# Softmax sums' small constant added on GpSimd one step sooner, high parts of six weight pieces rounded on GpSimd

## The chip, the core and the metric

The kernel runs on one core of a Trainium2 chip. TensorE (PE in the rows) multiplies (PEld are its weight loads); VectorE (DVE), ScalarE (ACT) and GpSimd (POOL) work element by element, SyncE (SP) issues most loads. Each engine runs its own instructions strictly in the order of the program; between engines, semaphores hold an instruction until what it needs is there. The metric is the device time of one execution in microseconds, as a median of several runs. Before the change it is 601.28 us (601.18 to 601.39).

## The reference

Banded attention with a few global keys is followed by two gated products, all in float32:

```python
scores = scale * np.matmul(q, k.transpose(0, 1, 3, 2)) + bias     # 2 batches, 8 heads, 768 rows, 64 wide
scores = np.where(keep, scores, -1e9)
a = np.exp(scores - np.max(scores, axis=-1, keepdims=True))
a = a / (np.sum(a, axis=-1, keepdims=True) + 1e-09)
x = np.matmul(a, v)                                               # 1536 rows x 512
x = ((x @ w1) * (x @ w2)) @ w3 @ w_out                            # d_ff 1024
out = ((x @ w_a) * (x @ w_b)) @ w_out2                            # d_ff 1536
```

The line that matters here is the fifth: the small constant 1e-09 is added to the row sums before they divide.

## The kernel before

The 1536 rows are 12 tiles of 128. A *unit* is one tile and two heads, so attention has 48 units of 128 rows x 2 heads x 256 keys (128 keys in the first tile of a batch). `band_attention` runs a loop of *steps* `u`; in step `u` it emits, in this order, for different units (the lag behind `u` in brackets): the scores on TensorE (`band_scores`, every second step, two units), the exponentials on ScalarE with their row sums `z` (`band_exp`, unit `u-2`), transposes on TensorE with a copy on ScalarE (`band_turn`, five or six units behind), the products with v (`band_values`), and then, dealt out in turns by `feed`, the row maxima on VectorE (`band_max`, unit `u-1`, two instructions at line 444) and the normalisation (`band_norm`, unit `u-3`). Before the change `band_norm` has three parts: VectorE adds EPS to `z` (line 465, 128x2 numbers), VectorE takes the reciprocal (line 467), and GpSimd multiplies the exponentials by it (line 469, two instructions of 128x256). As a generator that stops after the addition, it comes in two turns: the addition follows the first maximum, the reciprocal the second.

The same loop feeds weights. They come as 64-bit floats in *pieces* of 128x512; a piece that is begun in step `s` gets two ScalarE instructions then (lines 89 and 90), three on VectorE in step `s+1` (lines 94, 98 and 102), its *high part* rounded on ScalarE in step `s+2` (`upper`, line 115), and its low part subtracted on VectorE in step `s+3` (line 119). Pieces are begun in steps 3, 6, 9, 12, 14, 16, 20 and 24, and every fourth step from 36 on. Every fourth step from 20 on prepares a tile of keys and queries: ScalarE rounds the keys (line 368), GpSimd the queries (line 369, 128x1024, tile `qa`), and one step later VectorE subtracts both (lines 380 and 383). Steps 2 to 5 also have GpSimd make two of the eight heads' bias tables each (line 321). From step 15 on, matrix products of the first expert (`ab_band`, lines 669 to 671) are put between the steps on TensorE; each ends with a copy on ScalarE (line 677) and a product on VectorE (line 678). No scheduler moves anything: the order in which the Python code emits the instructions is each engine's order.

A step in which VectorE has only its two maxima, the addition and the reciprocal is called *light* below: steps 16, 18, 20, 22, 24, 34, 36, 38, 40 and some more.

Of the kernel before, what the change touches and what calls it, by code (L numbers as in the profile page):

```python
# [14 lines left out]
ALU = mybir.AluOpType  # L15
# [6 lines left out]
EPS = 1.0e-9  # L22
# [5 lines left out]
def f32(ap):  # L28
    return ap.bitcast(F32)


class Emitter:
# [74 lines left out]
    def convert(self, hi, lo, raw, g=None):  # L107


        nc = self.nc  # L110
        g = self.half("g", list(hi.shape)) if g is None else g
        words, join = self.doubles(g, raw)

        def upper():
            nc.scalar.copy(out=hi, in_=g)
            yield

        def rest():
            nc.vector.tensor_tensor(out=lo, in0=g, in1=f32(hi), op=ALU.subtract)
            yield  # L120

        return [words, join, upper, rest]
# [328 lines left out]
    def band_exp(self, u):  # L451
# [7 lines left out]
            )  # L459
        self.sm[u] = (s, z, lo)  # L460

    def band_norm(self, u):
        nc = self.nc
        s, z, lo = self.sm[u]
        nc.vector.tensor_scalar_add(z, z, EPS)
        yield
        nc.vector.reciprocal(z, z)  # L467
        for j in range(2):
            nc.gpsimd.tensor_scalar(  # L469
                out=s[:, j, lo:], in0=s[:, j, lo:], scalar1=z[:, j : j + 1], scalar2=1.0, op0=ALU.mult, op1=ALU.mult  # L470
            )
# [51 lines left out]
    def band_attention(self, filler):  # L523

        self.v, self.qs, self.sp, self.sm, self.pt, self.pv = ({} for _ in range(6))
        self.kq = dict(enumerate(self.kq01))
        self.ks = self.const.tile([P, 3, self.H, P], F32R, name=self.name("ks"))
        self.globs = self.const.tile([P, self.H, MAX_GLOBAL], F32, name=self.name("globs"))
        C = self.C
        nt = self.B * self.NB  # L530
        nu = nt * C
        self.patient = True
        masks = self.band_masks()
        self.feed_load(1, self.nc.scalar)
        next(masks)

        self.nc.vector.tensor_copy(out=self.nf, in_=self.ni.bitcast(U32))
        next(masks)
        block_stages = (
            (0, self.band_load_v), (C - 1, self.band_global), (-3, self.band_low), (-4, self.band_high), (-6, self.band_load),  # L540
        )
        early = sorted((C * t + lag, t, n) for t in range(nt) for n, (lag, _) in enumerate(block_stages) if C * t + lag < 0)
        for _, t, n in early:
            if t and n != len(block_stages) - 1:
                for _ in block_stages[n][1](t) or ():
                    pass
        spent = 0.0
        turned = valued = 0
        stores = {}
        u = -1  # L550
        while self.stored < nt:
            u += 1
            self.step = u
            at = lambda lag, stage: stage(u - lag) if 0 <= u - lag < nu else None
            at(0, self.band_scores)
            at(2, self.band_exp)
            while turned < min(nu, u - 4 if u < 16 else u - 5):
                self.band_turn(turned)
                turned += 1


            while valued < min(nu, u - 5 if u < 16 else u - 6) and (u < self.pairs_from or u % 4 == 2):
                self.band_values(valued)
                valued += 1
                if valued % C == 0:
                    for n, stage in enumerate((self.store_x, self.store_x_low, self.set_stored)):
                        stores.setdefault(u + n, []).append((stage, valued // C - 1))
            turns = [at(1, self.band_max), at(3, self.band_norm)]
            turns += [stage(t) for stage, t in stores.pop(u, ())]
            for lag, stage in block_stages:  # L570
                t, c = divmod(u - lag, C)
                if c == 0 and 0 <= t < nt:
                    turns.append(stage(t))
            self.feed([x for x in turns if x])
            if u:
                next(masks, None)
            for _ in range(2):
                if spent < 0.85 * (u - 14) - 0.15 * max(u - 38, 0):
                    spent += next(filler)
        self.patient = False  # L580
# [918 lines left out]
```

## Time and profile before

| | us |
|---|---|
| median of three runs | 601.28 |
| the profiled execution | 600.37 |
| its span, first to last instruction | 598.5 |
| TensorE busy in the span | 581.9 |
| VectorE busy | 446.2 |
| ScalarE busy | 366.3 |
| GpSimd busy | 171.3 |

The profile is of one execution. Its time is 1.87 us longer than its span, and 0.91 us shorter than the median. Attention takes the first 120 us; in the rest of the span TensorE's products follow each other. A row of a timeline gives the start, the duration, the engine, the line, and in brackets the idle time of the engine before it with what ended it. Back to back, an instruction starts before the one in front of it has ended, so the distance of two starts, not the duration, is what an instruction takes of its engine.

### The profile page before, as it was taken

What the parts mean: (1) busy time and instruction counts of PE and PEld (TensorE: products, weight loads), DVE (VectorE), ACT (ScalarE), POOL (GpSimd) and SP (SyncE); (2) the same over time, 40 slices, a digit from 0 to 9 for tenths busy, and PEclk for the clock granted to TensorE, in tenths of its full rate; (3) what the DMA queues carried; (4) which work ended last, traced back from release to release, by engine and by line L of the source; (5) the groups of instructions that cost most, each with busy time, mean ns of one, the idle gap of its engine ahead of it and who ended that gap; (6) DMA issues with size and microseconds to landing.
All of it is one profiled execution on the core that took longest, in us unless ns stands there. A gap on an engine that the chain in (4) does not pass through costs nothing.

```text
span 598.5 us, 10290 instructions
## 1 busy us (share of the span) xinstructions
PE 581.9 (97%) x3632; PEld 507.8 (85%) x3632; DVE 446.2 (75%) x974; ACT 366.3 (61%) x802; POOL 171.3 (29%) x226
## 2 busy tenths in 40 slices
PE   6989999999999999999999999999999999999996
PEld 4678997888888888888899888888888888889996
DVE  6897989539967483739999777777777789984781
ACT  5998889747745473648664444444444465895830
POOL 5655767500000000422612022222222221555500
PEclk9999999999999999999999999999999999999999
DMA  8999683326424322796714012122220248999941
GB/s 231 283 250 239 161 214 104 113 72 208 140 71 142 124 88 70 141 231 126 109 28 141 34 54 79 47 70 71 72 71 2 71 136 220 235 143 191 195 99 57
DMA packets 31821, 76.78 MB, mean 128 GB/s; under 512 B 3601, under 2 KB 11281, under 8 KB 31761
## 3 DMA queue, kind: packets, MB, share of 16 engines
q1 hardware_dynamic: 20560, 57.42, 32.2%
q0 software_dynamic: 10624, 17.83, 18.0%
q10 hardware_dynamic: 576, 0.79, 0.5%
q8 instruction: 30, 0.49, 0.4%
q14 instruction: 31, 0.25, 0.1%
HBM read 55.05 MB, written 3.15 MB: 97 GB/s over the span
## 4 chain that ended last, share of the span: by engine, by line
PE 87%; DVE 6%; ACT 3%; issue 2%; POOL 1%; POOLq 0%; DVEq 0%; ACTq 0%
PE ab_band L931 29%; PE o_band L931 16%; PE y_band L931 10%; PE ab_band L669 7%; PE ab_band L670 6%; PE ab_band L671 6%; PE wfp_band L244 2%; PE wfp_band L243 2%; PE wfp_band L245 2%; PE pv_band L516 2%; DVE s_band L444 2%; PE pt_band L480 2%; ACT s_band L456 1%; DVE qb_band L383 1%; PE sp_band L410 1%
## 5 line engine op out<-in xcount | busy, mean ns | idle before, releaser
L931 PE MATMUL ab_band<-y_band,ws_band 128*128 128x512 f32 (+1 forms) x576 | 110.2, 337 | 0.0
L931 PEld LDWEIGHTS ab_band<-y_band,ws_band 128*128 128x128 f32 x576 | 91.1, 190 | 12.0
L669 PE MATMUL ab_band<-xh_band,w_band 128*128 128x512 f32 (+1 forms) x216 | 81.8, 379 | 0.0
L671 PE MATMUL ab_band<-xh_band,w_band 128*128 128x512 f32 (+1 forms) x216 | 79.1, 366 | 0.0
L670 PE MATMUL ab_band<-xl_band,w_band 128*128 128x512 f32 (+1 forms) x216 | 79.0, 366 | 0.0
L469 POOL TENSOR_SCALAR s_band<-s_band,z_band 128x256 f32<-128x256 f32 (+1 forms) x96 | 61.0, 648 | 35.9 <-DVE z_band L467 15.4
L931 PE MATMUL o_band<-wo_band,gs_band 128*128 128x256 f32 (+1 forms) x360 | 59.1, 326 | 0.0
L931 PE MATMUL y_band<-gs_band,wf_band 128*128 128x512 f32 (+1 forms) x336 | 58.4, 336 | 0.0
L931 PEld LDWEIGHTS o_band<-wo_band,gs_band 128*128 128x128 f32 x360 | 53.1, 190 | 5.9
L931 PEld LDWEIGHTS y_band<-gs_band,wf_band 128*128 128x128 f32 x336 | 51.8, 190 | 6.6
L931 PE MATMUL ab_band<-y_band,wa_band 128*128 128x512 f32 (+1 forms) x288 | 56.4, 338 | 0.0
L90 ACT ACTIVATE raw_band<-raw_band 128x512 int32<-128x512 uint32 x76 | 51.2, 674 | 0.0
L931 PEld LDWEIGHTS ab_band<-y_band,wa_band 128*128 128x128 f32 x288 | 46.0, 190 | 6.1
L678 DVE TENSOR_TENSOR g_band<-ab_band,b_band 128x512 f32<-128x512 f32 (+1 forms) x27 | 16.9, 629 | 45.2 <-ACT b_band L677 45.2
L456 ACT ACTIVATE s_band<-s_band,m_band 128x256 f32<-128x256 f32 (+1 forms) x96 | 46.8, 495 | 3.6 <-DVE m_band L444 3.4
L669 PEld LDWEIGHTS ab_band<-xh_band,w_band 128*128 128x128 f32 x216 | 40.7, 188 | 7.6 <-issue 1.0
L671 PEld LDWEIGHTS ab_band<-xh_band,w_band 128*128 128x128 f32 x216 | 40.6, 188 | 6.6
L670 PEld LDWEIGHTS ab_band<-xl_band,w_band 128*128 128x128 f32 x216 | 40.8, 189 | 6.1
L1133 ACT COPY p_band<-ab_band 128x512 f32<-128x512 f32 (+1 forms) x48 | 22.1, 484 | 33.2 <-PE ab_band L931 33.0
L799 POOL DMA_DIRECT2D wq_band<-wq_band x4 | 4.6, 1156 | 125.5 <-DVE wf_band L812 124.4
L1134 DVE TENSOR_TENSOR u_band<-ab_band,u_band 128x512 f32<-128x512 f32 (+1 forms) x24 | 13.3, 555 | 33.1 <-PE ab_band L931 32.6
L444 DVE CUSTOM_DVE_ANT_0 s_band<-sp_band,bias_band 128x256 f32<-128x256 f32 (+1 forms) x96 | 37.3, 391 | 0.6 <-ACT bias_band L309 0.4
(160 smaller groups left out, 1262.5 us busy)
## 6 DMA issues: line engine op xcount, KB each, us to landing
raw_band<-in_moe_w_dram SPq DMA_DIRECT2D x31, 512.0 KB, 4.8
raw_band<-in_moe_w_out_dram SPq DMA_DIRECT2D x20, 512.0 KB, 4.4
raw_band<-in_moe_w_b_dram SPq DMA_DIRECT2D x12, 512.0 KB, 3.5
raw_band<-in_moe_w_a_dram SPq DMA_DIRECT2D x12, 512.0 KB, 4.5
ga_band<-ga_band POOLq DMA_DIRECT2D x24, 256.0 KB, 6.8
v_band<-in_v_dram SPq DMA_DIRECT2D x12, 256.0 KB, 7.7
kd_band<-in_kq_dram SPq DMA_DIRECT2D x12, 256.0 KB, 6.6
qd_band<-in_kq_dram SPq DMA_DIRECT2D x12, 256.0 KB, 7.0
```

The lines of the kernel that those rows point to most:

```text
L90: nc.scalar.activation(out=low, in_=low.bitcast(U32), func=AF.Copy, scale=2.0**-29)
L243: nc.tensor.matmul(acc, w[:, 1, k % 4, :], o[:, 0, 0, :], start=(k == 0), stop=False)
L444: nc.vector.tensor_tensor_reduce(out=s[:, j, lo:], in0=sp[:, j, lo:], in1=bias[:, 2 * c + j, :], scale=-self.scale, scalar=FLT_MAX, op0=AL ...
L456: nc.scalar.activation(out=s[:, j, lo:], in_=s[:, j, lo:], func=AF.Exp, bias=m[:, j : j + 1], scale=-1.0, accum_out=z[:, j : j + 1],)
L469: nc.gpsimd.tensor_scalar(out=s[:, j, lo:], in0=s[:, j, lo:], scalar1=z[:, j : j + 1], scalar2=1.0, op0=ALU.mult, op1=ALU.mult)
L669: nc.tensor.matmul(p, wl, xh, start=(c == 0), stop=False)
L670: nc.tensor.matmul(p, wh, xl, start=False, stop=False)
L671: nc.tensor.matmul(p, wh, xh, start=False, stop=(c == self.C - 1))
L678: nc.vector.tensor_tensor(out=out[:, at], in0=ps[0], in1=b, op=ALU.mult)
L931: self.nc.tensor.matmul(bank, wt, xt, start=start and i == n == 0, stop=stop and n == 2 and i == len(terms) - 1, skip_group_check=more,)
L1133: copy = lambda out: nc.scalar.copy(out=out, in_=bank)
L1134: plus = lambda t: nc.vector.tensor_tensor(out=t, in0=bank, in1=t, op=ALU.add)
```

## The change

The addition of EPS becomes a method of its own, `band_sum`, on GpSimd, for unit `u-2` in step `u`: the step in which ScalarE makes that unit's sums, one step before the addition stood. `band_norm` is no longer a generator and is called before the turns are dealt out, so reciprocal and multiplications of unit `u-3` come first in step `u`, the addition for unit `u-2` behind them. In steps before 22 of the attention loop, `upper` rounds on GpSimd and not on ScalarE; by the steps in which pieces are begun these are the roundings of steps 5, 8, 11, 14, 16 and 18.

```diff
--- before.py
+++ after.py
@@ -112,7 +112,10 @@
         words, join = self.doubles(g, raw)
 
         def upper():
-            nc.scalar.copy(out=hi, in_=g)
+            if self.patient and self.step < 22:
+                nc.gpsimd.tensor_scalar(out=hi, in0=g, scalar1=1.0, scalar2=1.0, op0=ALU.mult, op1=ALU.mult)
+            else:
+                nc.scalar.copy(out=hi, in_=g)
             yield
 
         def rest():
@@ -459,11 +462,14 @@
             )
         self.sm[u] = (s, z, lo)
 
+    def band_sum(self, u):
+
+        _, z, _ = self.sm[u]
+        self.nc.gpsimd.tensor_scalar(out=z, in0=z, scalar1=EPS, scalar2=1.0, op0=ALU.add, op1=ALU.mult)
+
     def band_norm(self, u):
         nc = self.nc
         s, z, lo = self.sm[u]
-        nc.vector.tensor_scalar_add(z, z, EPS)
-        yield
         nc.vector.reciprocal(z, z)
         for j in range(2):
             nc.gpsimd.tensor_scalar(
@@ -565,7 +571,9 @@
                 if valued % C == 0:
                     for n, stage in enumerate((self.store_x, self.store_x_low, self.set_stored)):
                         stores.setdefault(u + n, []).append((stage, valued // C - 1))
-            turns = [at(1, self.band_max), at(3, self.band_norm)]
+            at(3, self.band_norm)
+            at(2, self.band_sum)
+            turns = [at(1, self.band_max)]
             turns += [stage(t) for stage, t in stores.pop(u, ())]
             for lag, stage in block_stages:
                 t, c = divmod(u - lag, C)
```

GpSimd's queue in steps 2 to 6, where `z` are row sums, `s` a unit's exponentials, `bias` the tables of the heads, and `w` a weight piece. Before:

```order
L321 TENSOR_SCALAR bias_band_230<-dist_band_227 128x256 x2
L469 TENSOR_SCALAR s_band_258<-s_band_258,z_band_271 128x128 x2
L321 TENSOR_SCALAR bias_band_230<-dist_band_227 128x256 x2
L469 TENSOR_SCALAR s_band_277<-s_band_277,z_band_283 128x128 x2
L321 TENSOR_SCALAR bias_band_230<-dist_band_227 128x256 x2
L469 TENSOR_SCALAR s_band_287<-s_band_287,z_band_315 128x128 x2
L321 TENSOR_SCALAR bias_band_230<-dist_band_227 128x256 x2
L469 TENSOR_SCALAR s_band_322<-s_band_322,z_band_335 128x128 x2
```

And now:

```order
L468 TENSOR_SCALAR z_band_271<-z_band_271 128x2
L324 TENSOR_SCALAR bias_band_230<-dist_band_227 128x256 x2
L475 TENSOR_SCALAR s_band_258<-s_band_258,z_band_271 128x128 x2
L468 TENSOR_SCALAR z_band_284<-z_band_284 128x2
L324 TENSOR_SCALAR bias_band_230<-dist_band_227 128x256 x2
L475 TENSOR_SCALAR s_band_278<-s_band_278,z_band_284 128x128 x2
L468 TENSOR_SCALAR z_band_316<-z_band_316 128x2
L324 TENSOR_SCALAR bias_band_230<-dist_band_227 128x256 x2
L475 TENSOR_SCALAR s_band_292<-s_band_292,z_band_316 128x128 x2
L468 TENSOR_SCALAR z_band_336<-z_band_336 128x2
L116 TENSOR_SCALAR w_band_296<-g_band_297 128x512
L324 TENSOR_SCALAR bias_band_230<-dist_band_227 128x256 x2
```

Each unit's addition stands behind the multiplications of the unit in front of it, and the next pair of tables, and once a rounding, behind the addition.

VectorE's queue from the end of step 37 to the start of step 40, where `m` are row maxima, `ks` keys, `xl` low parts of the attention's output. Before:

```order
L678 TENSOR_TENSOR g_band_933<-ab_band_1446,b_band_1603 128x512
L444 ISA s_band_1651,m_band_1652<-sp_band_1526,bias_band_230 128x256
L444 ISA m_band_1652 128x1
L465 TENSOR_SCALAR z_band_1574<-z_band_1574 128x2
L444 ISA s_band_1651,m_band_1652<-sp_band_1526,bias_band_230 128x256
L444 ISA m_band_1652 128x1
L467 RECIPROCAL z_band_1574<-z_band_1574 128x2
L394 CAST ks_band_221<-globs_band_222 128x8x32
L444 ISA s_band_1671,m_band_1672<-sp_band_1606,bias_band_230 128x256
L444 ISA m_band_1672 128x1
L465 TENSOR_SCALAR z_band_1616<-z_band_1616 128x2
L498 TENSOR_TENSOR xl_band_1159<-pv_band_1626,xh_band_1158 128x2x128
```

And now:

```order
L686 TENSOR_TENSOR g_band_934<-ab_band_1447,b_band_1604 128x512
L473 RECIPROCAL z_band_1575<-z_band_1575 128x2
L447 ISA s_band_1656,m_band_1657<-sp_band_1527,bias_band_230 128x256
L447 ISA m_band_1657 128x1
L447 ISA s_band_1656,m_band_1657<-sp_band_1527,bias_band_230 128x256
L447 ISA m_band_1657 128x1
L473 RECIPROCAL z_band_1617<-z_band_1617 128x2
L397 CAST ks_band_221<-globs_band_222 128x8x32
L447 ISA s_band_1676,m_band_1677<-sp_band_1607,bias_band_230 128x256
L447 ISA m_band_1677 128x1
L504 TENSOR_TENSOR xl_band_1164<-pv_band_1627,xh_band_1163 128x2x128
L122 TENSOR_TENSOR w_band_1558<-g_band_1559,w_band_1558 128x512
```

The reciprocal is now the first instruction of its step; the maxima of the step stand behind it.

ScalarE's queue in steps 5 and 6, where `pt` are transposed exponentials. Before:

```order
L456 ACTIVATE s_band_322,z_band_335<-s_band_322,m_band_323 128x128 x2
L482 COPY pt_band_341<-pt_band_338 128x2x128
L115 CAST w_band_295<-g_band_296 128x512
L456 ACTIVATE s_band_343,z_band_364<-s_band_343,m_band_344 128x256 x2
L482 COPY pt_band_370<-pt_band_367 128x2x128
```

Line 115's row is gone from there and from five more places; the rest of ScalarE's order, and all of TensorE's, is as it was.

## Rows read from the trace of the kernel before

**Rows 1.** Busy time in stretches: stretch, sum, then engines, PE clock, DMA share, GB/s.

```profile
30.00:45.00 15.00, 13.46 (x138) 11.48 (x136) 14.37 (x57) 14.85 (x46) 8.83 (x13) 1.00 1.06 252
...
75.00:90.00 15.00, 15.00 (x113) 13.47 (x111) 12.64 (x50) 13.24 (x41) 9.63 (x15) 1.00 0.86 213
...
120.00:150.00 30.00, 30.00 (x161) 24.98 (x160) 19.59 (x35) 18.63 (x34) 0.00 (x0) 1.00 0.41 136
```

**Rows 2.** The chain that ended last, in order of time: start us, us, what.

```profile
49.98 0.33 DVE s_band L444
...
79.52 0.33 DVE s_band L444
...
105.68 0.33 DVE s_band L444
...
106.17 0.63 PE pt_band L480 x4
```

**Rows 3.** Groups of instructions, line 465: count, busy us, mean ns, idle before.

```profile
L465 DVE TENSOR_SCALAR z_band<-z_band 128x2 f32<-128x2 f32 x48 | 11.3, 234 | 1.5 <-ACT s_band L456 1.5
```

**Rows 4.** Lines 465 and 467: count, duration ns min/median/max, first and last start.

```profile
L465 DVE TENSOR_SCALAR z_band<-z_band x48: 156/166/822, 9.6 to 116.1; 128x2 f32<-128x2 f32 x48
...
L467 DVE RECIPROCAL z_band<-z_band x48: 153/156/167, 10.0 to 116.3; 128x2 f32<-128x2 f32 x48
```

**Rows 5.** Timeline of POOL at the start: start us, us, engine, line, operation, shapes, count, idle.

```profile
8.98 0.89 POOL L321 TENSOR_SCALAR bias_band<-dist_band 128x256 bf16<-128x256 f32 x2 [0.57 <-DVE dist_band L317]
...
11.30 1.66 POOL L321 TENSOR_SCALAR bias_band<-dist_band 128x256 bf16<-128x256 f32 x2
...
12.95 0.72 POOL L469 TENSOR_SCALAR s_band<-s_band,z_band 128x128 f32<-128x128 f32 x2
```

**Rows 6.** Timeline of DVE, steps 7 and 8.

```profile
14.99 0.35 DVE L394 COPY kq<-globs_band 128x128 f32<-128x128 f32 x1
...
18.60 0.16 DVE L467 RECIPROCAL z_band<-z_band 128x2 f32<-128x2 f32 x1
```

**Rows 7.** Timeline of ACT, steps 2 to 12.

```profile
8.59 0.19 ACT L456 ACTIVATION_READ_ACCUMULATOR s_band<-s_band,m_band 128x1 f32 x1
...
20.22 0.51 ACT L456 ACTIVATE s_band<-s_band,m_band 128x256 f32<-128x256 f32 x1
...
26.27 0.64 ACT L115 CAST w_band<-g_band 128x512 fp32r<-128x512 f32 x1
...
26.79 0.52 ACT L456 ACTIVATE s_band<-s_band,m_band 128x256 f32<-128x256 f32 x1
```

**Rows 8.** Timeline of DVE, step 21.

```profile
49.55 0.42 DVE L678 TENSOR_TENSOR g_band<-ab_band,b_band 128x256 f32<-128x256 f32 x1 [4.02 <-ACT b_band L677]
```

**Rows 9.** Timeline of DVE, steps 38 to 41.

```profile
92.92 0.41 DVE L444 CUSTOM_DVE_ANT_0 s_band<-sp_band,bias_band 128x256 f32<-128x256 f32 x1
...
93.26 0.17 DVE L465 TENSOR_SCALAR z_band<-z_band 128x2 f32<-128x2 f32 x1
...
93.67 0.16 DVE L467 RECIPROCAL z_band<-z_band 128x2 f32<-128x2 f32 x1
...
93.75 0.28 DVE L394 CAST ks_band<-globs_band 128x256 fp32r<-128x256 f32 x1
...
95.42 0.41 DVE L444 CUSTOM_DVE_ANT_0 s_band<-sp_band,bias_band 128x256 f32<-128x256 f32 x1
...
98.12 1.47 DVE L380 TENSOR_TENSOR ks_band<-kd_band,ks_band 64x1024 fp32r<-64x1024 f32 x1
```

**Rows 10.** Timeline of POOL, steps 38 to 40.

```profile
94.03 0.93 POOL L469 TENSOR_SCALAR s_band<-s_band,z_band 128x256 f32<-128x256 f32 x2 [1.28 <-ACT s_band L456]
...
97.01 1.05 POOL L369 TENSOR_SCALAR qa_band<-qd_band 128x1024 fp32r<-128x1024 f32 x1
```

**Rows 11.** Timeline of ACT, steps 39 and 40.

```profile
95.88 0.51 ACT L456 ACTIVATE s_band<-s_band,m_band 128x256 f32<-128x256 f32 x1 [0.37 <-DVE m_band L444]
...
96.85 1.05 ACT L368 CAST ks_band<-kd_band 128x1024 fp32r<-128x1024 f32 x1
```

## Prediction

> **What bounds the kernel now.** I read the busy time by stretches first. From 120 to 150 us TensorE is busy for all of 30.00 us [rows 1], and so it goes on: what attention delays by then, the rest of the kernel does not give back. The change touches attention alone, the first 120 us. There no single engine is the bound: from 30 to 45 us ScalarE is busy for 14.85 us of 15 and VectorE for 14.37, from 75 to 90 us TensorE for 15.00 [rows 1]. GpSimd, at 8.83 and 9.63 us, has room on average. Second, the chain of waits. It runs through VectorE's maxima around 50 us and from 79.52 to 105.68 us for most of the time, and reaches TensorE for good at 106.17 us [rows 2]. So a microsecond of VectorE or ScalarE is worth something here, and the question is not how busy GpSimd is but when it hands the sums back. Third, therefore, the timelines of the places where the new order binds.
>
> **The addition leaves VectorE.** Its 48 instructions are busy 11.3 us, 156 ns at least and 822 ns at most [rows 3, 4]. Back to back one takes less of the queue: in step 38 addition and second maximum lie between 93.26 and 93.67 us, 0.41 us, of which a maximum takes 0.34 (92.92 to 93.26) [rows 9]; the addition's share is 0.07 us.
>
> **The addition on GpSimd.** The trace has no 128x2 operation of GpSimd. Its multiplications take 0.72 us for two of 128x128 [rows 5] and 0.93 us for two of 128x256 [rows 10], so 0.36 and 0.465 each; 128 columns more cost 0.105 us, and with no columns 0.255 us are left. I take 0.26 us; the ends are nothing and the 0.36 us of the nearest row. The moved rounding has 512 columns: between 0.465 us for 256 and 1.05 us for the 1024 of line 369 [rows 10], which gives 0.66 us.
>
> **The new circle.** In the new order the reciprocal of unit n waits for GpSimd's addition for n, which stands in GpSimd's queue behind the multiplications of unit n-1, which wait for the reciprocal of n-1. Nothing of this went round before: VectorE added by itself, and GpSimd could fall behind without VectorE noticing. One turn of the circle costs 0.36 us from a reciprocal's start to the multiplications' (93.67 to 94.03), 0.93 us for the multiplications [rows 9, 10] and 0.26 us for the addition: 1.55 us. A light step keeps VectorE for 0.83 us (92.92 to 93.75) [rows 9], and now for 0.07 less. Wherever VectorE sets the pace, the reciprocal behind a light step makes it wait, with all its queue: the next maxima, low parts and joins. In steps with two or more microseconds of other VectorE work the circle is covered.
>
> **Term 1, the start.** Here GpSimd is behind already, with the tables. From the end of unit 0's sums (8.59 + 0.19 = 8.78 us) [rows 7] until the addition for unit 4 it must do five additions (1.30 us), four pairs of tables at 0.89 us (3.56), the multiplications of units 0 to 3 at 0.72 us (2.88) [rows 5] and one rounding (0.66): 8.40 us, until 17.2 us. One pair of tables took 1.66 us instead of 0.89 while VectorE worked on a weight piece [rows 5]; with one such delay it is 18.0 us. VectorE's step 7, which began at 14.99 us [rows 6], now begins with the reciprocal of unit 4, so it is 3.0 us late. It reached the end of step 8 at 18.60 + 0.08 us [rows 6], 3.7 us after 14.99; less two additions, that is now 21.5 us. The exponentials of unit 7 need that step's maxima; they began at 20.22 us [rows 7]. ScalarE is 1.3 us late there; without a delay by the weight piece 0.5 us, with three of them 2.8 us.
>
> **Term 2, steps 9 to 20.** Four of the six roundings lie behind that point, each worth the 0.52 us from 26.27 to 26.79 us [rows 7]: ScalarE alone would be at 1.3 - 2.1 = -0.8 us. VectorE carries its 3.0 us on, saves 11 additions (0.8 us) and waits behind the light steps 16, 18 and 20, 0.8 us each: 4.6 us late at step 21. There it had waited 4.02 us for ScalarE's copy [rows 8], which swallows all but 0.6 us. I take +0.6 us for what leaves step 21, between -0.8 (ScalarE decides) and +2.1 (the late start of term 1).
>
> **Term 3, the rest of attention.** In step 38 VectorE keeps 1.55 - 0.83 = 0.72 us more than before. In step 39 the reciprocal comes in front and the addition goes, which cancels; so the second maximum, at 95.42 us [rows 9], comes 0.72 us later. ScalarE waited for it (0.37 us idle in front of 95.88), and the rounding of the keys at 96.85 us [rows 11] follows it, for which line 380 waits at 98.12 us [rows 9]: the delay goes round. The same stands behind light steps 22, 34 and 42, on the stretches in which VectorE is the chain. Behind 36 and 40 the wait is hidden, as line 380 waits for ScalarE there anyhow, but the 1.05 us of line 369 [rows 10] now begin behind the addition and can hold line 380 up. Four times 0.72 us is 2.9 us; I take 2.4, since one of them may find ScalarE with some slack. TensorE, full in between and afterwards, passes it on. The bounds are 0 (all covered) and four times 1.0 us (with the delay by line 369).
>
> **The sum.** The profiled execution took 600.37 us, 1.87 more than its span. +0.6 and +2.4 make 603.4 us, and as the median lies 0.9 us above the profiled execution, 604.3 us.
>
> **The port.** The additions lost 11.3 - 48 x 0.156 = 3.8 us over their shortest time, while no reciprocal took more than 167 ns [rows 3, 4]: only the addition was held up. The Trainium skill (SBUF — State Buffer, "Who interferes with whom") says that VectorE and GpSimd share a port pair that one of them holds for a whole instruction, and that VectorE's scalar forms in a two-port mode ask for it. By that the move takes 48 requests away and the trace agrees with 822 against 167 ns; but the page has instructions with two SBUF inputs ask for it too. In the trace line 380, 1.47 us long at 98.12 us [rows 9], follows directly on the rounding of the queries that began at 97.01 and took 1.05 us [rows 10]: with the addition gone line 380 is the one that waits for it. So I take none of the 3.8 us; that some of them come back is part of the first rival.
>
> **Rivals.** *Faster.* ScalarE alone decides, because VectorE reaches its reciprocals late anyhow, or because GpSimd gets its work done during the maxima, when nothing disputes it. For it speak ScalarE's 14.85 of 15 us and that multiplications now start up to a step's length sooner, so that transposes find them ready; against it that VectorE is nearly as full. Then term 2 gives -0.8, term 3 nothing, and of the 3.8 us that additions lost half comes back, an estimate (the stretch from 79.52 to 105.68 us [rows 2] alone is a quarter of attention): -2.7 us, 598.6. It decides if a turn of the circle costs no more than a light step, 0.83 us. *No change.* The waits behind light steps fall into gaps that TensorE's products leave, and roundings saved pay for the late start: 601.3. TensorE's 15.00 of 15 us speak for it, the chain through VectorE up to 105.68 us against it. *Much slower.* The start is late by three delays, which term 2 passes on as +2.1, and each loop of term 3 loses 1.0 us: +6.1, 607.4 us. For it speaks that GpSimd's multiplications and line 380 dispute each other already; against it that multiplications now lie under the maxima.
>
> **How the numbers follow.** My forecast has a chance of 0.42 (own range 602.5 to 606), much slower 0.16, no change 0.20, faster 0.22. A change of 0.2%, 1.2 us, is about what a measurement of this kernel can tell: faster 0.22, same 0.20, slower 0.58. The range, 599.5 to 607.5 us, takes in the upper bounds and half of the faster case.
>
> **What would show it.** Right: VectorE idle in front of reciprocals, ended by GpSimd's addition, some 0.7 us behind light steps and 1 us or more in steps 4 to 7; VectorE in step 7 near 18 us; GpSimd's 128x2 addition near 0.26 us; TensorE's stretch without gaps beginning 2 to 4 us after 106. Wrong: reciprocals that start without a wait, or a wait at step 21 that has not shrunk from 4.02 us. If ScalarE shows gaps in 20 to 45 us, the roundings bought nothing; if it stays full and ends earlier, the faster case holds.

## The result, and the profile after

The changed kernel takes 608.92 us (median of 4 runs, 608.69 to 609.05) against 601.23 us for the kernel before (600.46 to 601.39), a ratio of 1.0134, 95% interval 1.0122 to 1.0146. It is 7.7 us slower; 3.0 were forecast, and the time lies outside the range. The profiled execution took 609.05 us with a span of 607.3. The first product of line 939, which starts when attention and the first expert are done, and everything after it come 8.27 us later than before: all of the loss lies in attention, as forecast.

The stretches that answer to [rows 1], and one more (columns as there; the first stretch had 14.02, 10.06, 12.93, 13.81, 10.30 before, at a clock of 1.00 by the view):

```profile
15.00:30.00 15.00, 11.74 (x82) 8.35 (x84) 10.48 (x42) 11.63 (x37) 10.75 (x24) 0.66 1.06 289
30.00:45.00 15.00, 14.30 (x159) 11.78 (x156) 12.48 (x44) 13.23 (x41) 11.75 (x23) 1.00 1.05 253
75.00:90.00 15.00, 14.53 (x131) 12.96 (x130) 11.93 (x40) 12.80 (x42) 12.50 (x22) 1.00 0.72 185
120.00:150.00 30.00, 30.00 (x193) 25.11 (x192) 14.94 (x37) 19.03 (x44) 4.19 (x11) 1.00 0.39 128
```

From 30 to 45 us VectorE went from 14.37 to 12.48 us and ScalarE from 14.85 to 13.23, while GpSimd rose from 8.83 to 11.75: neither of the two is full any more. From 75 to 90 us TensorE has lost its 15.00 of 15, and from 120 us on it is full as before. What ended the waits of the first 135 us (engine, line, what it waited for: us in total, times, longest):

```profile
DVE z_band L473 <- POOL z_band L468: 17.9, 23, 1.5
ACT s_band L459 <- DVE m_band L447: 11.6, 18, 1.3
...
PE sp_band L430 <- DVE ks_band L397: 4.1, 3, 2.2
```

The first row is the forecast wait: 23 of 48 reciprocals idle VectorE for 17.9 us. The second is the next engine in line, the third is TensorE behind VectorE's copy of the global keys. Before the change these two were:

```profile
ACT s_band L456 <- DVE m_band L444: 3.4, 6, 1.0
...
PE sp_band L427 <- DVE ks_band L394: 1.4, 1, 1.4
```

One turn of the circle, on VectorE and then on GpSimd (start us, us):

```profile
59.42 0.16 DVE L473 RECIPROCAL z_band<-z_band 128x2 f32<-128x2 f32 x1
...
60.98 0.17 DVE L473 RECIPROCAL z_band<-z_band 128x2 f32<-128x2 f32 x1 [0.73 <-POOL z_band L468]
...
63.34 0.16 DVE L473 RECIPROCAL z_band<-z_band 128x2 f32<-128x2 f32 x1
...
64.90 0.17 DVE L473 RECIPROCAL z_band<-z_band 128x2 f32<-128x2 f32 x1 [0.73 <-POOL z_band L468]
```

```profile
63.66 0.93 POOL L475 TENSOR_SCALAR s_band<-s_band,z_band 128x256 f32<-128x256 f32 x2 [0.63 <-DVE z_band L473]
64.68 0.19 POOL L468 TENSOR_SCALAR z_band<-z_band 128x2 f32<-128x2 f32 x1
64.95 1.05 POOL L372 TENSOR_SCALAR qa_band<-qd_band 128x1024 fp32r<-128x1024 f32 x1
```

From reciprocal to reciprocal 1.56 us, with 0.32 us from the reciprocal's start to the multiplications', 1.02 to the addition's start, 0.22 to the next reciprocal. The addition is busy 0.19 us and takes 0.27 of the queue.

The chain that ended last goes round this circle, and reaches TensorE for good at 114.43 us, where it was 106.17 [rows 2]:

```profile
99.49 0.08 DVE z_band L473
...
100.19 0.49 POOL s_band L475
100.75 0.20 POOL z_band L468
...
101.25 0.42 DVE s_band L447
...
111.35 0.49 POOL s_band L475
111.91 0.20 POOL z_band L468
112.22 0.27 DVE ks_band L397
...
114.43 0.63 PE pt_band L486 x4
```

At the start, step 7 on VectorE, then ScalarE's exponentials of unit 7, then TensorE's scores of units 8 and 9 (before: 14.99 [rows 6], 20.22 [rows 7], and 16.70 without a wait):

```profile
18.96 0.17 DVE L473 RECIPROCAL z_band<-z_band 128x2 f32<-128x2 f32 x1 [1.51 <-POOL z_band L468]
19.08 0.23 DVE L397 COPY kq<-globs_band 128x128 f32<-128x128 f32 x1
```

```profile
22.36 0.51 ACT L459 ACTIVATE s_band<-s_band,m_band 128x256 f32<-128x256 f32 x1
```

```profile
19.36 0.80 PE L413 MATMUL sp_band<-kq,kq_band 64*128 64x128 f32 x4 [3.11 <-DVE kq L397]
```

And step 21, where VectorE meets ScalarE's copy of the first expert. Before, VectorE's product came at 49.55 us after a wait of 4.02 [rows 8], and the copy here:

```profile
49.12 0.40 ACT L677 ACTIVATE b_band<-ab_band 128x256 f32<-128x256 f32 x1
```

In the changed kernel, two of the exponentials in front of the copy, the copy, and VectorE's product:

```profile
46.91 0.51 ACT L459 ACTIVATE s_band<-s_band,m_band 128x256 f32<-128x256 f32 x1 [0.60 <-DVE m_band L447]
...
50.40 0.51 ACT L459 ACTIVATE s_band<-s_band,m_band 128x256 f32<-128x256 f32 x1 [0.72 <-DVE m_band L447]
...
53.46 0.36 ACT L685 ACTIVATE b_band<-ab_band 128x256 f32<-128x256 f32 x1
```

```profile
53.86 0.42 DVE L686 TENSOR_TENSOR g_band<-ab_band,b_band 128x256 f32<-128x256 f32 x1 [2.41 <-ACT b_band L685]
```

Where the delay is made shows in the starts of the exponentials (first of the two of a unit): their start before, and how much later they start in the changed kernel and in some of the experiments below (in the order of the columns: e2, e8, e10, e6, e5, e1 and e14 of the table there). Each number is the difference of two rows of ScalarE's timelines, each from one execution.

| unit | before, us | changed | sum only | head, VectorE | sum first | early units | late units | round only | two operations |
|---|---|---|---|---|---|---|---|---|---|
| 4 | 13.40 | 1.01 | 0.84 | 0.74 | 0.08 | 0.86 | -0.17 | -0.12 | 1.62 |
| 9 | 24.81 | 3.17 | 2.19 | 0.42 | 1.67 | 2.42 | -0.34 | -0.29 | 3.64 |
| 18 | 44.68 | 4.39 | 2.27 | 0.52 | 1.59 | 2.30 | 1.23 | -0.90 | 7.39 |
| 30 | 75.50 | 6.16 | 4.15 | 2.12 | 1.47 | 2.30 | 3.01 | -0.17 | 10.61 |
| 43 | 107.03 | 8.26 | 6.58 | 3.22 | 1.77 | 2.29 | 5.35 | -0.16 | 14.93 |

So 4.4 us are lost by unit 18 and 3.9 between units 18 and 43. How far single executions can differ shows in e17, which runs the same instructions as the changed kernel up to step 13: its delay is 2.52 us at unit 9 and 3.08 at unit 11, where the changed kernel has 3.17 and 3.62. Differences of half a microsecond in this table therefore show nothing by themselves.

### The profile page after: what moved, and what is told of

It is laid out like the page before. It is cut to its first block, busy times and chain, and to the rows that moved or that the text cites. A ratio compares the mean times of both kernels' runs of the same rounds, so it can differ in the third digit from the quotient of the medians.

```text
span 607.3 us, 10319 instructions
## 1 busy us (share of the span) xinstructions
PE 584.8 (96%) x3632; PEld 510.4 (84%) x3632; DVE 443.2 (73%) x926; ACT 365.5 (60%) x796; POOL 183.0 (30%) x280
## 4 chain that ended last, share of the span: by engine, by line
PE 81%; DMA 8%; DVE 4%; issue 2%; POOL 2%; ACT 1%; SPq 1%; DVEq 0%; POOLq 0%; ACTq 0%
PE ab_band L939 29%; PE o_band L939 15%; PE y_band L939 10%; PE ab_band L677 6%; PE ab_band L679 6%; PE ab_band L678 6%; DMA kd_band<-in_kq_dram 3%; PE wfp_band L246 2%; DMA v_band<-in_v_dram 2%; PE wfp_band L248 2%; PE wfp_band L247 2%; DMA kq_band<-in_kq_dram 2%; POOL s_band L475 1%; PE pv_band L522 1%; PE pt_band L486 1%
## 5 line engine op out<-in xcount | busy, mean ns | idle before, releaser
L475 POOL TENSOR_SCALAR s_band<-s_band,z_band 128x256 f32<-128x256 f32 (+1 forms) x96 | 53.5, 568 | 27.1 <-DVE z_band L473 19.2
L774 POOL TENSOR_TENSOR sf_band<-gb_band 128x256 f32<-128x256 f32 x12 | 10.3, 861 | 95.2 <-DVE gb_band L102 76.3
```

The costliest lines, as they stand in the source:

```text
L475: nc.gpsimd.tensor_scalar(out=s[:, j, lo:], in0=s[:, j, lo:], scalar1=z[:, j : j + 1], scalar2=1.0, op0=ALU.mult, op1=ALU.mult)
```

## The experiments

Theory: the circle reciprocal, multiplications, next addition, next reciprocal makes the loss, since the reciprocal stands at the head of VectorE's step. The rivals are named in the expectations. Times are medians; the interval is that of the ratio to the kernel before, measured beside it on the same chip. From one such group of kernels to the next the median of the kernel before varied from 600.37 to 601.23 us, so a difference of about 1 us between kernels of different groups is read from the delays at unit 43 as well.

| kernel | us | before, us | ratio | 95% |
|---|---|---|---|---|
| e1_round_only | 600.04 | 601.19 | 0.9985 | 0.9976 to 0.9993 |
| e2_sum_only | 607.16 | 601.19 | 1.0108 | 1.0093 to 1.0123 |
| e8_head_vector | 603.53 | 601.19 | 1.0052 | 1.0039 to 1.0065 |
| e7_recip_last | 600.45 | 601.19 | 0.9995 | 0.9987 to 1.0004 |
| e10_sum_first | 602.47 | 600.56 | 1.0037 | 1.0025 to 1.0049 |
| e4_copy_first | 608.19 | 600.56 | 1.0128 | 1.0113 to 1.0142 |
| e5_late_units | 606.13 | 600.56 | 1.0094 | 1.0081 to 1.0107 |
| e6_early_units | 603.52 | 600.56 | 1.0055 | 1.0042 to 1.0068 |
| e14_two_ops | 614.79 | 600.67 | 1.0235 | 1.0221 to 1.0249 |
| e11_head_no_sum | 599.31 | 600.67 | 0.9981 | 0.9971 to 0.9991 |
| e12_recip_last_act | 601.45 | 600.67 | 1.0010 | 1.0001 to 1.0019 |
| e13_round_all | 599.37 | 600.67 | 0.9981 | 0.9970 to 0.9991 |
| e16_sum_first_act | 604.94 | 600.37 | 1.0074 | 1.0060 to 1.0088 |
| e17_round_12 | 608.31 | 600.37 | 1.0131 | 1.0115 to 1.0146 |
| e15_apart | 600.58 | 600.37 | 1.0002 | 0.9993 to 1.0011 |
| e18_apart_round | 603.21 | 600.37 | 1.0047 | 1.0033 to 1.0061 |

**The two halves apart.** First the roundings alone, from the kernel before:

```diff
-            nc.scalar.copy(out=hi, in_=g)
+            if self.patient and self.step < 22:
+                nc.gpsimd.tensor_scalar(out=hi, in0=g, scalar1=1.0, scalar2=1.0, op0=ALU.mult, op1=ALU.mult)
+            else:
+                nc.scalar.copy(out=hi, in_=g)
```

> The kernel before with the second half of the change alone: six roundings on GpSimd. Theory (the circle: the reciprocal at the head of VectorE's step waits for an addition that stands behind GpSimd's multiplications): no circle here, so 600.0 to 602.0 us, TensorE's gapless stretch beginning within 1 us of 106.2, no reciprocal waiting for GpSimd. Rival A (the roundings load GpSimd in the first 40 us, and the rest follows): 604 to 609 us, most of the 8.3 us of delay of the changed kernel. Rival B (order alone: the reciprocal in front of the maxima) and rival C (the additions dispute VectorE's port): 599.5 to 601.5 us, as for the theory.

600.04 us, 1.1 us faster than before by the medians and 0.16 by the delay at unit 43: rival A falls by either. Second, the changed kernel without that edit:

> The changed kernel with its roundings back on ScalarE: the additions on GpSimd and the reciprocal first, nothing else. Theory: nearly the whole loss stays, 606 to 609 us; VectorE's waits for GpSimd's addition at 14 to 19 us in sum, the scores near 19 us waiting 2 us or more for the copy of the keys. Rival A: the loss goes, 601 to 603.5 us. Rivals B and C: the loss stays, 606 to 609 us.

607.16 us, and VectorE's waits for GpSimd's addition are 16.6 us in 23 places: the additions make the loss. The roundings, a gain of at most 1.1 us alone, cost 1.8 us on top of them (1.7 by the delays).

**Circle or order.** The addition back on VectorE, at the place of the changed kernel's reciprocal; `band_sum` is not called, and the roundings are on ScalarE:

```diff
     def band_norm(self, u):
+        nc.vector.tensor_scalar_add(z, z, EPS)
         nc.vector.reciprocal(z, z)
...
             at(3, self.band_norm)
-            at(2, self.band_sum)
```

> The order of the changed kernel (reciprocal in front of the maxima, multiplications earlier in GpSimd's queue), but the addition stays on VectorE, directly in front of the reciprocal; roundings on ScalarE. Theory: no wait of VectorE for GpSimd, so 599.5 to 602.5 us and scores near 16.7 to 17.5 us. Rival B (order alone): 606 to 609 us. Rival C (GpSimd's additions dispute the port): 600 to 602 us.

603.53 us: without the circle 3.6 of the 6.0 us of `e2_sum_only` are gone (3.4 by the delays, 6.58 to 3.22), but 2.3 stay, more than the theory allowed. Then the changed kernel with its two calls swapped, so that GpSimd's addition stands in front of the multiplications and the circle is open:

```diff
-            at(3, self.band_norm)
             at(2, self.band_sum)
+            at(3, self.band_norm)
```

> The changed kernel with two calls of the loop swapped: the addition for unit u-2 is emitted in front of the normalisation of unit u-3. On GpSimd the addition now stands in front of the multiplications, so the circle is open; the reciprocal stays first in VectorE's step, and all else stays. Theory (the circle costs most of the start's loss and a smaller part later, the early reciprocal some 2.4 us by itself, as with the addition on VectorE): 601.5 to 605 us; VectorE's waits for GpSimd's addition fall from 17.9 us in sum to below 6. Rival C (additions on GpSimd are dear in themselves, by the port or by GpSimd's load): 606 to 609 us.

602.47 us, and VectorE's waits, in the first 135 us:

```profile
DVE z_band L473 <- POOL z_band L468: 4.6, 7, 1.3
```

The same instructions on the same engines, one pair of neighbours exchanged on GpSimd, and the kernel is 6.4 us faster than the changed one (608.92 - 602.47; 6.5 by the delays). Rival C falls. It falls again where the reciprocal goes back behind the second maximum as well:

```diff
-            at(3, self.band_norm)
             at(2, self.band_sum)
-            turns = [at(1, self.band_max)]
+            turns = [at(1, self.band_max), at(3, self.band_norm)]
```

with a `yield` ahead of the reciprocal:

> Both parts of the change, but the reciprocal and the multiplications stay behind the second maximum, where they stood before; so GpSimd's addition for unit n+1 stands in front of the multiplications of unit n and the circle is open. Theory: the additions are done by the time the reciprocal comes, 599.5 to 602.5 us, waits of reciprocals for GpSimd below 3 us in sum after the first 20 us. Rival A (GpSimd's load) and rival C (its port): the loss stays for the most part, 605 to 609 us. Rival B (order): 600 to 602 us.

600.45 us, no difference from before that can be measured. With its roundings back on ScalarE:

> Additions on GpSimd one step sooner with the reciprocal and the multiplications in their old place, and the roundings left on ScalarE: the first half of the change without the circle. Theory: VectorE's 0.07 us in 48 places are saved and nothing waits, 599 to 601.5 us. Rival C (additions on GpSimd dear in themselves): 602 us and more.

601.45 us. Taking 48 additions from VectorE, 11.3 us of busy time [rows 3], is worth nothing here.

**What the place at the head costs.** The version with addition and reciprocal both at the head, and its light step from 87.81 us on:

```profile
87.81 0.17 DVE L471 RECIPROCAL z_band<-z_band 128x2 f32<-128x2 f32 x1
...
88.57 0.16 DVE L470 TENSOR_SCALAR z_band<-z_band 128x2 f32<-128x2 f32 x1
88.77 0.17 DVE L471 RECIPROCAL z_band<-z_band 128x2 f32<-128x2 f32 x1
```

The reciprocal follows its addition after 0.20 us, where addition and reciprocal apart take 0.07 and 0.08 of the queue [rows 9]; the step is 0.96 us long instead of 0.83. Two kernels test whether this pair or the place matters. The addition left out:

```diff
-            at(2, self.band_sum)
```

> Reciprocal first in VectorE's step and multiplications early, as in the changed kernel, but the addition of the small constant is left out altogether (it is part of the computation that this kernel does not do); roundings on ScalarE. Theory G (the reciprocal's place costs nearly nothing; what the version with addition and reciprocal at the head lost between units 20 and 43, 2.7 us, is the reciprocal's wait for the addition directly in front of it, 0.20 us from start to start instead of 0.07): 599.5 to 601.7 us, light steps of 0.83 us or less. Rival B (the place in front of the maxima costs it): 602.5 to 604 us.

599.31 us, 0.2 below the range. And the addition first in the step, the reciprocal behind the first maximum (from the kernel before; `band_norm` is the one of before, with a `yield` between the two):

```diff
+            first = at(3, self.band_norm)
+            next(first or iter(()), None)
-            turns = [at(1, self.band_max), at(3, self.band_norm)]
+            turns = [at(1, self.band_max), first]
```

> The addition and the reciprocal stay on VectorE; the addition is first in the step, the reciprocal and the multiplications come behind the first maximum; roundings on ScalarE. The version with both in front (603.53 us) differs only in that the reciprocal follows its addition directly. Theory G (a dependent instruction directly behind costs 0.13 us more, 0.20 instead of 0.07 from start to start): 599.8 to 601.8 us, light steps 0.83 us. Rival B (the place): 602.5 to 604 us.

600.58 us, with the light step from 93.18 to 94.00 us:

```profile
93.18 0.16 DVE L470 TENSOR_SCALAR z_band<-z_band 128x2 f32<-128x2 f32 x1
93.25 0.42 DVE L444 CUSTOM_DVE_ANT_0 s_band<-sp_band,bias_band 128x256 f32<-128x256 f32 x1
93.59 0.16 DVE L472 RECIPROCAL z_band<-z_band 128x2 f32<-128x2 f32 x1
...
94.00 0.16 DVE L470 TENSOR_SCALAR z_band<-z_band 128x2 f32<-128x2 f32 x1
```

With the addition on VectorE or left out rival B falls: the place in front of the maxima costs nothing that can be measured, the dependent pair directly behind each other does, some 0.1 us in each step. That the dependence does it, and not the meeting of two tiny instructions, shows in larger ones in the kernel before. Line 98 works on the result of line 94 and starts 0.46 us behind it, a maximum, which does not, 0.33:

```profile
10.66 0.43 DVE L94 TENSOR_SCALAR g_band<-g_band 128x512 int32<-128x512 int32 x1
11.12 0.74 DVE L98 SCALAR_TENSOR_TENSOR g_band<-raw_band,g_band 128x512 int32<-128x512 int32 x1
...
15.67 0.42 DVE L94 TENSOR_SCALAR g_band<-g_band 128x512 int32<-128x512 int32 x1
16.00 0.41 DVE L444 CUSTOM_DVE_ANT_0 s_band<-sp_band,bias_band 128x256 f32<-128x256 f32 x1
```

**Where the delay is made.** The new order for the units from 9 on alone, and for units 0 to 8 alone; the other units as before the change (in the second the two conditions are exchanged; `band_norm_before` is the old `band_norm`):

```diff
+            early = lambda v: self.band_norm(v) if v >= 9 else None
+            plain = lambda v: None if v >= 9 else self.band_norm_before(v)
-            at(3, self.band_norm)
-            at(2, self.band_sum)
-            turns = [at(1, self.band_max)]
+            at(3, early)
+            at(2, lambda v: self.band_sum(v) if v >= 9 else None)
+            turns = [at(1, self.band_max), at(3, plain)]
```

> The changed kernel, but units 0 to 8 have their addition on VectorE and their reciprocal behind the second maximum, as before the change; from unit 9 on as changed. Theory (the delay is made in two places, about 4.4 us by unit 18 and 3.9 us between units 21 and 43): the second part stays, 603.5 to 606 us, the first exponentials of unit 18 within 1.5 us of before. Rival E (all comes from the start, and the rest only passes it on): 599.5 to 602 us.

> The other half: the new order for units 0 to 8 alone, and from unit 9 on the addition on VectorE and the reciprocal last, as before the change; roundings on GpSimd up to step 21. Theory (two places that add up): 602.5 to 605.5 us, with 2 to 4 us of delay at unit 9 and no more than that at the end, some of it given back as VectorE finds slack. Rival E (all from the start): 606.5 to 609 us.

606.13 and 603.52 us, 5.6 and 3.0 us above before. By the delays at unit 43 the two places add up: 5.35 + 2.29 = 7.64 of 8.26 us. Rival E falls twice, and a detail of the theory too: hardly anything of the early delay is given back, 2.42 us at unit 9, 2.30 at unit 18 and 2.29 at unit 43. The first kernel lies 0.1 us above its range, since it loses 1.23 us already by unit 18.

Next the copy for TensorE's scores: `band_global` is called ahead of `band_norm` instead of behind it.

```diff
...
+            at(C - 1, lambda v: self.band_global(v // C) if v % C == 0 else None)
             at(3, self.band_norm)
```

> The changed kernel with one edit: VectorE's copy of the global keys (line 397), which stood behind the waiting reciprocal, is emitted in front of it, in one step of four. Circle, additions and roundings stay. Theory (part of the loss comes through this copy, for which TensorE's next scores wait: 3.1 us at 19.36, 1.1 at 48.70, 4.1 us in sum at line 430): scores of units 8 and 9 wait below 1.2 us, the time falls by 1.5 to 4 us to 605 to 607.5 us. Rival D (the copy only passes on a delay that the maxima behind the reciprocal suffer anyway): 608 to 609.5 us.

608.19 us, 0.7 us below the changed kernel (7.54 against 8.26 at unit 43). TensorE's scores of units 8 and 9 now start 1.76 us sooner:

```profile
17.60 0.80 PE L413 MATMUL sp_band<-kq,kq_band 64*128 64x128 f32 x4 [1.40 <-DVE kq L397]
```

and the exponentials of unit 18 are still 4.05 us late instead of 4.39. The theory's range is missed and rival D holds: the copy passes on a delay that the maxima suffer anyway.

**The size of a turn.** A second operation of the same kind on GpSimd:

```diff
         self.nc.gpsimd.tensor_scalar(out=z, in0=z, scalar1=EPS, scalar2=1.0, op0=ALU.add, op1=ALU.mult)
+        self.nc.gpsimd.tensor_scalar(out=z, in0=z, scalar1=1.0, scalar2=1.0, op0=ALU.mult, op1=ALU.mult)
```

> The changed kernel with GpSimd's 128x2 operation doubled: after the addition a second one multiplies the sums by 1. One turn of the circle becomes 0.27 us longer (the spacing of such operations on GpSimd). Theory (the circle sets the pace behind light steps and in the start): about 18 waits of 0.7 us grow by 0.27 us each, of which roughly half to all reaches TensorE: 611 to 614 us, single waits near 1.0 us, turns near 1.83 us. Rival F (VectorE's waits lie in slack, and the loss comes through clock, copies or loads): 608.5 to 610 us.

614.79 us, 5.9 us above the changed kernel (6.7 by the delays) and 0.8 above the theory's range; 27 waits instead of 23:

```profile
62.44 0.16 DVE L474 RECIPROCAL z_band<-z_band 128x2 f32<-128x2 f32 x1
64.30 0.17 DVE L474 RECIPROCAL z_band<-z_band 128x2 f32<-128x2 f32 x1 [1.03 <-POOL z_band L469]
```

A turn is 1.86 us, 0.30 more, and 48 tiny operations cost 5.9 us on an engine that was busy for 183.0 of the changed kernel's 607.3 us, and for 82.0 of the first 120, in which nearly all of them stand. Rival F falls.

**Why the roundings turn round.** The version with the swapped calls, roundings on ScalarE; and the changed kernel with GpSimd rounding only up to step 11 (`self.step < 12`):

> The version with the addition in front of the multiplications on GpSimd (circle open, 602.47 us), with its roundings back on ScalarE. Theory H (with the circle closed a rounding stands between an addition and the next multiplications and makes a turn 0.6 us longer; with the circle open it only relieves ScalarE): without the roundings this version is slower by about 1 us, 602.8 to 604.2 us. Rival I (roundings on GpSimd cost in any order of additions): 600 to 602 us.

> The changed kernel, but with GpSimd rounding only the pieces of steps 5, 8 and 11; those of steps 14, 16 and 18 are back on ScalarE. Theory H: between the version without roundings (607.16) and the changed kernel (608.92), 607.2 to 608.5 us; the delay at units 11 and 12 as in the changed kernel (3.6 us), but not growing to 4.4 by unit 18. Rival I: half of it too, so time cannot tell them apart here, only where the delay grows.

604.94 us, 0.7 above the range: with the circle open the roundings on GpSimd are worth 2.5 us (1.9 by the delays, 3.66 to 1.77), so rival I falls.

The same run sets a limit to what was said of the circle and of the place. With the roundings on ScalarE the exchange of the two calls is worth 2.2 us (607.16 to 604.94; 2.9 by the delays), not 6.4. And with the circle open, the reciprocal first in the step takes 604.94 us where the reciprocal last takes 601.45; with the roundings on GpSimd it is 602.47 against 600.45. These are 3.5 and 2.0 us (3.4 and 1.5 by the delays) for the place of reciprocal and multiplications in front of the maxima, which is free only while the addition is on VectorE or left out: a reciprocal that comes first still meets unfinished additions of GpSimd. In the version with 604.94 us these are 10 waits and 5.8 us, among them 0.99 and 1.08 us in steps 6 and 7, where the addition stands behind tables. Half of its 3.7 us of delay is there by unit 9 (1.82); what makes the other half no run takes apart.

With the circle closed the first three roundings cost 1.15 us (607.16 to 608.31; 1.1 by the delays). What the other three cost is not shown: the two kernels are 0.6 us apart, but 0.54 of that is there at unit 11 already, where the delay was 3.08 us, not 3.6, and where they still run the same instructions. At unit 18 it was 3.45 where the changed kernel's is 4.39. That a rounding lengthens a turn shows in the changed kernel's queue, in the start:

```profile
15.49 0.19 POOL L468 TENSOR_SCALAR z_band<-z_band 128x2 f32<-128x2 f32 x1
15.77 0.62 POOL L116 TENSOR_SCALAR w_band<-g_band 128x512 fp32r<-128x512 f32 x1
16.46 1.37 POOL L324 TENSOR_SCALAR bias_band<-dist_band 128x256 bf16<-128x256 f32 x2
17.93 0.72 POOL L475 TENSOR_SCALAR s_band<-s_band,z_band 128x128 f32<-128x128 f32 x2
18.74 0.19 POOL L468 TENSOR_SCALAR z_band<-z_band 128x2 f32<-128x2 f32 x1
```

Rounding, tables and multiplications stand between two additions; the last row is what the reciprocal at 18.96 us waited for.

**A better version.** The roundings of all attention's pieces on GpSimd, additions as before (the first diff without `and self.step < 22`), and the same with the addition apart:

> The kernel before with the high parts of all weight pieces of attention rounded on GpSimd, not only those of the first 22 steps. If ScalarE's queue is part of the path throughout: 598.5 to 599.8 us. If VectorE and TensorE decide from unit 25 on, where the version with six roundings had given back all but 0.16 us of its 1.4 us: 599.8 to 601 us. If GpSimd's longer roundings (0.62 us for 0.52) hold VectorE's subtractions up: 601 to 603 us.

> The version before with all pieces of attention rounded on GpSimd. If earlier multiplications (the version without the addition ran 1.4 us faster than before) and roundings on GpSimd (1.3 us faster) add up: 598 to 599.3 us. If both only take the same slack: 599.3 to 600.5 us.

599.37 us, 0.2% below before: the lowest ratio of the kernels that compute everything, though by its time (0.9981) it cannot be told from the one with six roundings (0.9985). It falls into the first case: the delay at unit 43 is -0.82 us, so what six roundings had given back by then (-0.16) is kept. The second kernel, 603.21 us, is slower than either of its parts, against both expectations. Its delay is made at units 17, 23, 39 and 43, and why is not settled.

## Why the prediction was wrong

**Right.** The direction; *the new circle* with its turn (1.55 us forecast, 1.56 measured) and its wait (0.72 against 0.73), where the close sum is in part luck, since its terms were 0.32, 1.02 and 0.22 us instead of 0.36, 0.93 and 0.26; *the addition on GpSimd* (0.26 us against a spacing of 0.27; the rounding 0.66 against 0.62); that TensorE is full behind attention and passes all on.

**Term 1** forecast VectorE's step 7 at 18.0 us and ScalarE 1.3 us late; it was 18.96 and 2.1 (22.36 - 20.22), inside the bounds of 0.5 to 2.8. GpSimd was held up not once but three times up to then: tables took 1.37 us (above) where 0.89 was priced, one unit's multiplications 1.30 for 0.72 (at 11.90 us), an addition 0.56 (at 13.29). And the circle does not end there: reciprocals waited again in steps 9, 10, 12 and 13, and the delay was 3.17 us at unit 9.

**Term 2 is the step that failed.** It made of 4.6 us of late VectorE 0.6, because VectorE had waited 4.02 us at step 21 [rows 8], and it let ScalarE gain 2.1 us by four roundings. Measured at step 21: VectorE begins to wait at 51.45 us (53.86 - 2.41) where it was 45.53 (49.55 - 4.02), 5.9 us late, and the wait takes up 1.6 us of that, not 4.0: the copy that it waits for comes 4.34 us later too (49.12 to 53.46), and VectorE's product 4.31 us later. The copy stands in ScalarE's queue behind exponentials that wait for VectorE's maxima (0.60 and 0.72 us in the rows above). The 4.02 us were slack against ScalarE's own work, but for the most part none against VectorE's delay, which came back through ScalarE. So 2.4 of the 3.7 us that term 2 is short at step 21 are the overlap that was not there, and 1.3 that VectorE came later than forecast. The kernel with the additions alone shows it without the roundings: 2.27 us late at unit 18, and 2.31 at its copy in step 21:

```profile
51.43 0.37 ACT L682 ACTIVATE b_band<-ab_band 128x256 f32<-128x256 f32 x1
```

And with its gaps ScalarE could not cash in the roundings: alone they bring 1.1 us (0.2 by the delays), with the circle open 2.5 (1.9), with it closed they lengthen the turns. So the +0.6 that were to leave step 21 were 4.3 us; the upper bound of 2.1 had the same error in it.

**Term 3** had the right wait and the wrong count. It took four waits, behind light steps 22, 34, 38 and 42, as *36 and 40* were to be hidden (both waits came, 0.74 us each), and did not count 24, 28 and 30. One row under it was misread: line 380 at 98.12 us names no wait for ScalarE; VectorE's addition in front of it, from 97.32 us on, took 0.76. Nine reciprocals waited from step 23 to TensorE's full stretch at 114.43 us, seven of them for 0.73 or 0.74 us (60.98 and 64.90 above, the last at 112.14), one for 0.79 and one for 0.52: 6.4 us, of which 3.9 reached TensorE. Forecast 2.4, upper bound 4.0.

**The port.** None of the 3.8 us was to come back, and nothing shows that any did: the version with the reciprocal last and ScalarE's roundings is not faster than before. On GpSimd the additions were held up in their turn: busy for 17.0 us, 7.8 more than 48 times their shortest, 0.191.

**Rivals.** *Much slower* had the nearest sum, 607.4 us, with the start's three delays and each loop at 1.0 us; the measured way is larger in term 2 and smaller in each wait. *Faster* and *No change* would have needed the circle open: with the two calls swapped the kernel is 1.9 us above before.

## What to carry to other kernels

When a small operation moves to another engine, draw the circles that the new handoffs close through in-order queues, and take the queue position of the operation, not its duration: one exchange of neighbours was worth 6.4 us here (2.2 with the roundings on ScalarE), the operation itself is 0.19 us long. A wait of engine A for engine B covers a delay of A only as far as B's work does not itself hang on A. An engine with room that stands inside such a circle is not spare: what is put on it lengthens the turn.

## What the runs showed of the hardware

A VectorE instruction of 128x2 that needs the result of the one directly in front of it starts 0.20 us after it, 0.07 us after an independent one (88.57 to 88.77, and 93.18 to 93.25 in the version with both apart); between larger ones the difference is the same 0.13 (0.46 and 0.33).

A copy of 128x128 on VectorE can take three times as long. The changed kernel's line 397, the same shape twice:

```profile
28.85 0.21 DVE L397 COPY kq_band<-globs_band 128x128 f32<-128x128 f32 x1
...
48.01 0.64 DVE L397 COPY kq_band<-globs_band 128x128 f32<-128x128 f32 x1
```

At the first GpSimd is idle, the second lies beside a rounding of GpSimd (from 47.95 us, 0.62 long). The other way round, the addition on GpSimd has a median of 191 ns and a maximum of 1222:

```profile
L468 POOL TENSOR_SCALAR z_band<-z_band x48: 191/191/1222, 8.9 to 124.8; 128x2 f32<-128x2 f32 x48
...
87.11 1.22 DVE L386 TENSOR_TENSOR qb_band<-qd_band,qa_band 128x1024 fp32r<-128x1024 f32 x1
...
87.16 1.22 POOL L468 TENSOR_SCALAR z_band<-z_band 128x2 f32<-128x2 f32 x1
```

Fourteen of the 48 took 0.50 us or more. Each of them starts 0.05 to 0.41 us behind a VectorE instruction with two tiles as inputs (lines 98, 102, 122 and 386) and ends 0.05 us behind it.

The Trainium skill (SBUF — State Buffer, "Who interferes with whom") says that copies too can ask for the port pair that VectorE shares with GpSimd, and that whoever comes second is blocked for the whole instruction; 0.64 us against 0.21 agrees with it.

TensorE's granted clock was 0.66 from 15 to 30 us in the changed kernel: 1.00 from 16 to 18 us, 0.50 from 20 to 28. It fell while TensorE waited 3.11 us, up to 19.36. The groups of scores of units 10 and 11 start 0.43 us apart there (24.87 to 25.30), later ones 0.22 (29.90 to 30.12): the 1.2 and the 2.4 GHz level. For the kernel before the view gives 1.00 in the same stretch, but its scores of units 8 and 9 start 0.43 us apart as well (17.28 to 17.71), and 0.22 only from units 10 and 11 on (21.69 to 21.91); so the two kernels differ by less than 0.66 and 1.00 say. The clock is no large term of the loss: four executions of the changed kernel, with mean granted clocks from 0.987 to 0.999, took 608.69 to 609.05 us, and the version with the reciprocal last had 0.77 from 15 to 30 us and took 600.45.
